# A one-element exponential ahead of the score exponentials, and the transposes of the smallest score tile moved behind the second vs product

## The chip, the cores and the metric

The kernel runs on one core of a Trainium2 chip. The metric is the device time of one execution in microseconds (us); a kernel's time is the median of several runs. Engines are named as in the profile: PE is TensorE's matrix multiplication and PEld its weight load, ACT is ScalarE, DVE is VectorE, POOL is GpSimd, SP is SyncE, which here issues most of the DMAs.

## What is computed

Three stages follow each other for 8 batches of 576 tokens with 512 features, all in float32:

```python
# 1: attention in two steps, 8 heads of 64
p_packed = sm_attn(p, k, v)                 # 32 packed queries per head
x = sm_attn(q, p_packed, p_packed)          # back to 576 tokens
# 2: a gated MLP that mixes tokens
h = gelu_tanh(x @ w_in)                     # 1024 features
u, v = h[..., :512], h[..., 512:]
v_n = (v - mean(v)) / sqrt(var(v) + 1e-6) * g_ln
v_s = einsum('ts,bsd->btd', w_sg, v_n) + b_sg
x = x + (u * v_s) @ w_out
# 3: four attention experts, causal; each token takes the best two of them by x @ w_gate
out = sum over experts of mask * w * (softmax(causal(q k^T / 8)) @ v) @ wo
```

## The kernel before, in words

Products that need accuracy are made of three passes over a high and a low part of each operand (`PASSES`), so PE has much to do. Tokens are cut into four tiles of 128 and one of 64 (`NT`, `TOK`). PSUM is one pool of four two-bank buffers (`pd`), which all products share.

Batches are worked in a software pipeline. `front(b)` makes the normalised v_n of batch b: it multiplies v out, runs gelu, mean and variance, scaling and the split into parts tile by tile, with the u products in between, and ends with `E0 E2`, which belong to the batch before: the scores and exponentials of stage 3. `later_back(b)` (batches 1 to 7) then makes the vs product (v_n with w_sg, four column tiles m of five parts c each) and the gate u * vs of batch b, interleaved with the rest of the attention of batch b - 1, and afterwards the q, k, v of batch b's stage 3 and the packed attention of the next one.

The names of the steps of stage 3: E are scores, causal mask, maximum and exponentials; N is the scaling by the reciprocal of the sum and the expert's weight; T turns the result with PE transposes and copies it out of PSUM on ACT; y is the product with v; o is the output projection. For the first two query tiles both head pairs are done together: E0, N0 and T0 are the 128-column tile, E2, N2 and T2 the 256-column tile (`att_exp2`, `att_norm2`, `att_T2`). Line 1013 holds their score products, 1015 the mask, 1018 the maximum, 1022 the exponentials, 1028 and 1029 the sums, 1031 the scalings, and 1041 the transposes; their copy is recorded at the helper's line 82, as are all plain ACT copies. N0 has four scalings and T0 four transposes with one copy; N2 has four and T2 eight with two.

What sets the order: on PE and SP the order is that of the program text through the whole main loop. In `front` it is so on DVE and ACT as well (`tc.manual_schedule(engines={ET.DVE, ET.Activation})`). In `later_back` DVE and ACT are ordered by the planner of the framework, which simulates the program and takes the ready instruction that stands earliest in the text, save in the few blocks marked otherwise. Waits between engines are put in by the framework. ACT holds one table of functions at a time: gelu's or the exponential's; the load of a table is an instruction of its own that is put ahead of the first activation that needs it, and has that activation's line. Per batch there are two: at line 722 (gelu) and at line 1022 (exponential).

The last steps of `front` on ACT are the scaled copies of the 64-token tile into its high and low part (lines 747 and 749). `vs_part` (lines 820, 824, 826) makes one part c of one column tile m: six matmuls for c below 4 and four for c = 4. `vs_out` multiplies by u on DVE (843), copies the high part on ACT (849) and makes the low part on DVE (helper line 85). `mhalf` is a constant column of -0.5.

Of the kernel before, what the change touches and what calls it, by code (L numbers as in the profile page):

```python
# [7 lines left out]
F32 = mybir.dt.float32  # L8
# [5 lines left out]
AF = mybir.ActivationFunctionType  # L14
# [3 lines left out]
P = 128  # L18
# [8 lines left out]
def packed_attention_mlp_moe_kernel(  # L27
# [18 lines left out]
    nc = tc.nc  # L46
# [6 lines left out]
    NT = 5  # L53
# [5 lines left out]
    small = ctx.enter_context(tc.tile_pool(name="small", bufs=4))  # L59
# [14 lines left out]
    def pd(name):  # L74

        return psum.tile([P, 2, 512], F32, tag="pd", name=name, bufs=NPS)
# [10 lines left out]
    def hs(h):  # L87
        return slice(h * HALF, (h + 1) * HALF)
# [17 lines left out]
    mhalf = consts.tile([P, 1], F32, name="mhalf")  # L106
# [246 lines left out]
    def prep_w_o(j):  # L353
        hi, lo = W["w_o"]
        st = wst.pop(("o", j))
        act_copy(hi[:, j, :], st)
        lo_part(nc.vector, lo[:, j, :], st, hi[:, j, :])
# [27 lines left out]
    def tick(n=1):  # L385
        for _ in range(min(n, len(TURN))):
            for f in TURN.pop(0):
                f()
# [274 lines left out]
    def bdw(b):  # L663
        bdw_qk(b)
        bdw_vg(b)
# [23 lines left out]
    def v_mm(b, pt, c):  # L689
        s = ST[b]  # L690
        n = 0
        if c == 4:
            for y in range(2):
                for Q in range(2):
                    nc.tensor.matmul(pt, s["a2", Q][0][:, 512:640], wp_part(b, 1, y, Q), start=n == 0, stop=n == 3)
                    n += 1
            return
        for x, y in PASSES:
            for Q in range(2):
                nc.tensor.matmul(pt, s["a2", Q][x][:, c * P:(c + 1) * P], wp_part(b, 1, y, Q), start=n == 0, stop=n == 5)  # L700
                n += 1

    def v_gelu(b, pt, c):
        if c == 4:
            v_sum_high(b, pt)
            v_sum_low(b, pt)
            v_sum_gelu(b)
            return
        vg = ST[b]["vg", c] = slot("t", w=512, name="vg")
        nc.scalar.activation(vg, pt, AF.Gelu_apprx_tanh)  # L710

    def v_sum_high(b, pt):
        vg = ST[b]["vg", 4] = slot("t", w=512, name="vg")[:64]
        act_copy(vg, pt[64:])

    def v_sum_low(b, pt):
        vg = ST[b]["vg", 4]
        nc.vector.tensor_tensor(vg, vg, pt[:64], op=OP.add)

    def v_sum_gelu(b):  # L720
        vg = ST[b]["vg", 4]
        nc.scalar.activation(vg, vg, AF.Gelu_apprx_tanh)
# [80 lines left out]
    def vs_tile(b, m):  # L803
        vs_mm(b, m)
        vs_out(b, m)

    def vs_mm(b, m):
        for c in range(NT):
            vs_part(b, m, c)

    def vs_part(b, m, c):
        s = ST[b]
        cols = slice(m * P, (m + 1) * P)
        if c == 0:
            s["vs", m] = pd("vs")[:, :, :HALF]
        pt = s["vs", m]
        if c < 4:
            for x, y in PASSES:
                for h in range(2):
                    nc.tensor.matmul(pt[:, h, :], s["vn", c][x][:, cols], w_sg[y][:, c, hs(h)],  # L820
                                     start=(c, x, y) == (0, 0, 0), stop=False)
            return
        for h in range(2):
            nc.tensor.matmul(pt[:, h, :], s["vn", 4][0][:, cols], w_sg[0][:, 4, hs(h)], start=False, stop=False)
        for h in range(2):
            nc.tensor.matmul(pt[:, h, :], s["vn", 4][1][:66, cols], w_sg[1][:66, 4, hs(h)], start=False, stop=True)
# [7 lines left out]
    def vs_out(b, m):  # L834
        gate_mul(b, m)
        gate_high(b, m)
        gate_low(b, m)
# [18 lines left out]
    def qk(b, i):  # L856
        qk_mm(b, i)
        qk_out(b, i)
# [6 lines left out]
    def qk_gated(b, i, first, ms=range(4)):  # L865
        s = ST[b]
        if first:
            s["qkp", i] = pd("qk")[:, :, :HALF]
        o = s["qkp", i]
        cols = slice(i * P, (i + 1) * P)  # L870
        for m in ms:
            for x, y in PASSES:
                for h in range(2):
                    nc.tensor.matmul(o[:, h, :], W["w_qk"][y][:, m, cols], s["g", m][x][:, hs(h)],  # L874
                                     start=first and (m, x, y) == (0, 0, 0), stop=not first and (m, x, y) == (3, 1, 0))

    def qk_packed(b, i, first):
        s = ST[b]
        if first:
            s["qkp", i] = pd("qk")[:, :, :HALF]  # L880
        o = s["qkp", i]
        cols = slice(i * P, (i + 1) * P)
        for Q in range(2):
            for x, y in PASSES:
                for h in range(2):
                    nc.tensor.matmul(o[:, h, :], s["bd", Q][y][:, cols], s["a2", Q][x][:, hs(h)],  # L886
                                     start=first and (Q, x, y) == (0, 0, 0), stop=not first and (Q, x, y) == (1, 1, 0))
# [12 lines left out]
    def keep_last_q(b, pr):  # L900
        for z, t in zip(last_q[pr], ST[b]["qk", pr]):
            for e in range(2):
                r = slice(64 * e, 64 * e + 64)
                nc.gpsimd.tensor_copy(z[r, r], t[r, 4 * P:S])

    def gate_beside(b):
        for m in range(4):
            t = ST[b]["gx", m]
            nc.gpsimd.tensor_copy(t[:, S:S + 64], t[:, 2 * S:])  # L909
# [309 lines left out]
    def weights(b, names):  # L1219
        if b < B:  # L1220
            for n in names:
                load_w(n)

    def front(b, go):

        with tc.manual_schedule(engines={ET.DVE, ET.Activation}):
            p4 = pd("v")[:, 0, :]
            v_mm(b, p4, 4)
            v_sum_high(b, p4)
            tick()  # L1230
            p = [None] * 4
            for c in range(4):
                if c % 2 == 0:
                    t = pd("v")
                p[c] = t[:, c % 2, :]
                v_mm(b, p[c], c)
                if c == 1:
                    v_sum_low(b, p4)
                    v_sum_gelu(b)
                    tick()  # L1240

            def run(names):
                fs = dict(g=lambda b, c: v_gelu(b, p[c], c), b=v_stats, p=v_pow, c=v_scale, h=v_high, l=v_low, U=u_mm,
                          u=u_gelu)
                for n in names.split():
                    if n == "t":
                        tick()
                    else:
                        fs[n[0]](b, int(n[1]))

            run("b4 g0 g1 b0 p0 c0 b1 p1 c1 h0 l0 U0 t")
            run("g2 g3 b2 p2 h1 c2 u0 l1 U1 t b3 p3 p4 c3 u1 U2 t h2 l2 u2 U3 t c4 h3 l3 u3 h4 l4")
            go("E0 E2")

    def second(b, do_all):
        do_all("r")
        for f in (1, 0):
            wp_mm(b, f)
        for f in (1, 0):
            wp_out(b, f)  # L1260
# [28 lines left out]
    def later_back(b, go, do_all, nxt):  # L1289
        go("N0 N2")  # L1290
        vs_tile(b, 0)
        for c in range(3):
            vs_part(b, 1, c)
        go("T0")
        for c in range(3, NT):
            vs_part(b, 1, c)
        with tc.manual_schedule(engines={ET.Activation}):
            go("T2")
            vs_out(b, 1)
        go("y0")  # L1300
        if b == 1:
            for j in range(2):
                prep_w_o(j)
        go("S5 S4")
        vs_tile(b, 2)
        go("o0 y1 T5 T4 S6 S7")
        vs_tile(b, 3)
        tick(len(TURN))
        if b + 1 < B:
            STEP.pop((b + 1, "f"))()  # L1310
        go("o1 y2")
        bdw(b)
        weights(b + 1, ("in1", "in0"))
        qk(b, 0)
        do_all("V T6 o2 T7 K0 S8 S9 K1")
        keep_last_q(b, 0)
        gate_beside(b)
        qk_gated(b, 2, True)
        with tc.manual_schedule(engines={ET.DVE}):
            do_all("s0 s1 n0 n1")  # L1320
        qk_packed(b, 2, False)
        qk_out(b, 2)
        if b + 1 == B:
            go("y3 T8 T9 o3 y4")
            nxt("E8")
            go("o4")
            vlog(b, VT[1])
            nxt("E6")
            vlog(b, VT[2])
            nxt("E4")  # L1330
            return
        do_all("y3 T8 T9 o3 a0 a1 y4 pp Q0 Q1 o4 P0 P1")
        vlog(b, VT[1])
        second(b + 1, do_all)
        vlog(b, VT[2])
        if b + 2 < B:
            ahead(b + 2)
# [43 lines left out]
    def ahead(b):  # L1381

        do(p1_steps(b))
# [255 lines left out]
    with tc.manual_schedule(engines={ET.PE, ET.SP}):  # L1639
        go = back(0, attention(-1))  # L1640
        for b in range(1, B):
            front(b, go)
            go = back(b, go)
# [31 lines left out]
```

## Time and profile before

| | us |
|---|---|
| median of 3 runs (lowest to highest) | 823.51 (823.33 to 825.58) |
| the profiled execution | 824.52 |
| its span, first to last instruction | 822.8 |
| PE busy in the span | 792.6 |
| DVE, ACT, POOL busy in the span | 586.8, 428.4, 229.3 |

The profile is of one execution. Times in it run from the start of the span. In a row of the timeline the columns are start, length, engine, line and operation, with the output and the input; rows of several instructions (x4) give the time from the start of the first to the end of the last. What stands in brackets is the idle time of the engine just before, and the instruction that ended it. The ends of matmuls are modelled, so their starts are the better marks.

### The profile page before, as it was taken

Reading aid. Unit: us, or ns where it says so; the run is one execution under the profiler, and the core shown is the slowest. Engines: PE = TensorE matmul, PEld = TensorE weight load, DVE = VectorE, ACT = ScalarE, POOL = GpSimd, SP = SyncE. Lnnn points to the kernel's source line nnn. Section 1 sums busy time; section 2 is a strip of 40 time slices with the busy share of each in tenths; the row PEclk is TensorE's granted clock in tenths of the full one; section 3 lists DMA queues with packets and bytes.
Section 4 is the critical chain, followed back from the end, with each engine's and each line's share of the span. In section 5 each row is a group of like instructions: output and inputs, shape, how many; then the busy total and the mean of one; then the engine's idle time right before and its main releaser. Section 6 shows DMA issues by size and latency. Waiting matters only on the chain.

```text
span 822.8 us, 19132 instructions
## 1 busy us (share of the span) xinstructions
PE 792.6 (96%) x7459; PEld 689.4 (84%) x7459; DVE 586.8 (71%) x1321; ACT 428.4 (52%) x947; POOL 229.3 (28%) x346
## 2 busy tenths in 40 slices
PE   4789899999999999999999999999999999999998
PEld 2457778988899888988899888988899888988886
DVE  4898567886488756886488757886488747885383
ACT  3566343665347543665347543575347543565454
POOL 2356443403331222403331222403331232300000
PEclk9979999999999999999999999999999999999999
DMA  9977889507582475607682476607672372000001
GB/s 236 292 201 166 241 252 228 142 14 223 153 196 73 102 232 158 161 18 221 149 199 74 105 231 173 149 15 221 155 194 73 97 238 85 1 15 26 21 1 58
DMA packets 172709, 114.99 MB, mean 140 GB/s; under 512 B 119306, under 2 KB 153610, under 8 KB 169804
## 3 DMA queue, kind: packets, MB, share of 16 engines
q1 hardware_dynamic: 165644, 112.19, 50.5%
q10 hardware_dynamic: 6976, 1.58, 0.9%
q8 instruction: 59, 0.97, 0.5%
q14 instruction: 30, 0.25, 0.1%
HBM read 69.18 MB, written 29.63 MB: 120 GB/s over the span
## 4 chain that ended last, share of the span: by engine, by line
PE 71%; DVE 12%; ACT 9%; DMA 3%; issue 3%; POOL 1%; SPq 0%; ACTq 0%; DVEq 0%; POOLq 0%
PE qk L874 13%; PE vs L820 7%; PE y L1124 7%; PE qk L886 6%; PE o L1173 5%; PE vlog L933 5%; PE aTp L1095 3%; PE sc L991 3%; PE vlog L937 3%; DVE bnst L728 2%; PE s L395 2%; ACT vnh L747 2%; DMA k<-in_k_dram 2%; PE aTp L1041 2%; PE sc L1068 2%
## 5 line engine op out<-in xcount | busy, mean ns | idle before, releaser
L874 PE MATMUL qk<-g,w_qk 128*128 128x288 f32 x768 | 107.4, 297 | 0.4 <-ACT a L490 0.4
L874 PEld LDWEIGHTS qk<-g,w_qk 128*128 128x128 f32 x768 | 103.4, 189 | 4.3 <-issue 2.9
L820 PE MATMUL vs<-w_sg,vnh 128*128 128x288 f32 x512 | 92.0, 302 | 1.5 <-ACT vs L82 1.5
L820 PEld LDWEIGHTS vs<-w_sg,vnh 128*128 128x128 f32 x512 | 74.8, 189 | 8.3 <-issue 5.6
L82 ACT ACTIVATE aT<-aTp 128x512 f32<-128x512 f32 (+4 forms) x125 | 55.8, 512 | 18.0 <-PE aTp L1041 9.1
L909 POOL CAST g<-g 128x64 fp32r<-128x64 f32 x32 | 9.0, 284 | 195.2 <-DVE g L85 93.3
L482 POOL COPY qT<-qp 128x576 uint16<-128x576 uint16 x56 | 43.0, 838 | 60.6 <-DMA qp<-turned_q 60.5
L1124 PE MATMUL y<-aT,v 128*64 128x128 f32 (+2 forms) x960 | 58.3, 263 | 1.0 <-ACT aT L82 0.9
L1001 ACT ACTIVATE at<-sc,nm 128x384 f32<-128x384 f32 (+3 forms) x72 | 43.4, 609 | 30.2 <-DVE nm L995 26.3
L1124 PEld LDWEIGHTS y<-aT,v 128*64 128x64 f32 (+1 forms) x960 | 46.8, 136 | 13.3 <-issue 8.3
L820 PE MATMUL vs<-w_sg,vnl 128*128 128x288 f32 x256 | 54.7, 295 | 0.0
L933 PE MATMUL vlog<-w_vg,g 128*128 128x260 f32 x384 | 52.1, 285 | 0.0
L736 POOL TENSOR_TENSOR rstd<-rstd,mhalf 128x1 f32<-128x1 f32 (+1 forms) x40 | 34.7, 868 | 56.8 <-DVE rstd L732 46.9
L1173 PE MATMUL o<-w_o,y 128*128 128x512 f32 x186 | 49.4, 401 | 0.0
L933 PEld LDWEIGHTS vlog<-w_vg,g 128*128 128x128 f32 x384 | 48.4, 189 | 1.2 <-PE wp L620 0.8
L482 POOL COPY kT<-kp 128x576 uint16<-128x576 uint16 x56 | 44.7, 876 | 8.9 <-DMA kp<-turned_k 8.9
L886 PE MATMUL qk<-a2h,bdq 128*128 128x288 f32 x256 | 45.4, 299 | 0.5 <-DVE sm L548 0.4
L820 PEld LDWEIGHTS vs<-w_sg,vnl 128*128 128x128 f32 x256 | 41.0, 188 | 0.0
L886 PEld LDWEIGHTS qk<-a2h,bdq 128*128 128x128 f32 x256 | 37.2, 188 | 4.5 <-issue 3.9
L85 DVE TENSOR_TENSOR y<-y 128x256 fp32r<-128x256 f32 (+1 forms) x40 | 15.9, 397 | 33.8 <-ACT y L1137 33.8
L1173 PEld LDWEIGHTS o<-w_o,y 128*128 128x128 f32 x186 | 32.9, 188 | 5.9 <-issue 0.5
L995 DVE TENSOR_REDUCE nm<-sc 128x2 f32<-128x768 f32 (+3 forms) x36 | 37.1, 1030 | 1.0
(264 smaller groups left out, 1895.6 us busy)
## 6 DMA issues: line engine op xcount, KB each, us to landing
w_in<-kept_in SPq DMA_DIRECT2D x14, 1024.0 KB
w_qk<-kept_qk SPq DMA_DIRECT2D x8, 1024.0 KB
turned_k<-kx SPq DMA_DIRECT2D x28, 288.0 KB
turned_q<-qx SPq DMA_DIRECT2D x28, 288.0 KB
kp<-turned_k SPq DMA_DIRECT2D x56, 144.0 KB
qp<-turned_q SPq DMA_DIRECT2D x56, 144.0 KB
out_dram<-ot SPq DMA_DIRECT2D x31, 256.0 KB
v<-in_v_dram SPq DMA_DIRECT2D x56, 128.0 KB
```

The costliest lines, as they stand in the source:

```text
L82: nc.scalar.activation(o, i, AF.Copy, scale=scale)
L482: nc.gpsimd.tensor_copy(w[:, i], t[:, i].rearrange("p h n -> p (h n)"))
L736: nc.gpsimd.tensor_tensor(rstd, rstd, mhalf[:TOK[c]], op=OP.pow)
L820: nc.tensor.matmul(pt[:, h, :], s["vn", c][x][:, cols], w_sg[y][:, c, hs(h)], start=(c, x, y) == (0, 0, 0), stop=False)
L874: nc.tensor.matmul(o[:, h, :], W["w_qk"][y][:, m, cols], s["g", m][x][:, hs(h)], start=first and (m, x, y) == (0, 0, 0), stop=not first an ...
L886: nc.tensor.matmul(o[:, h, :], s["bd", Q][y][:, cols], s["a2", Q][x][:, hs(h)], start=first and (Q, x, y) == (0, 0, 0), stop=not first and ...
L933: nc.tensor.matmul(pt[:, ci, :260], s["g", m][x][:, c * P:c * P + P], W["w_vg"][y][:, m, :], start=(m, x, y) == (0, 0, 0), stop=False)
L937: nc.tensor.matmul(pt[:, ci, :260], s["a2", Q][x][:, c * P:c * P + P], s["bdv", Q][y], start=False, stop=(Q, x, y) == (1, 1, 0))
L995: nc.vector.tensor_reduce(nm, pt[:, :, :L], axis=AX.X, op=OP.max, negate=True)
L1001: nc.scalar.activation(ats[e][:, :L], pt[:, e, :L], AF.Exp, bias=nm[:, e:e + 1], accum_out=sm[:, e:e + 1])
L1124: nc.tensor.matmul(pt[64 * e:64 * e + 64, pr * w:pr * w + w], s["v2"][:m, c, col:col + D], s["aT", pr, e, j][c][:m, :], start=c == 0, stop ...
L1173: nc.tensor.matmul(pt, ys[:, pr, x, :], W["w_o"][y][:, pr, :], start=i == 0, stop=i == 5)
```

## The change

Two edits. Behind the steps of the 64-token tile in `front` and ahead of the exponentials of E0, ACT computes an exponential of one column with one element per partition (`mhalf`), whose result nobody reads. In `later_back`, the transposes T0, which stood between the third and the fourth part of the second vs product (m = 1), come behind its fifth part, directly ahead of T2, and their copy stands with that of T2 in the block whose ACT order is that of the text.

```diff
             run("g2 g3 b2 p2 h1 c2 u0 l1 U1 t b3 p3 p4 c3 u1 U2 t h2 l2 u2 U3 t c4 h3 l3 u3 h4 l4")
+            warm = small.tile([P, 2], F32, name="st3")[:, 0:1]
+            nc.scalar.activation(warm, mhalf, AF.Exp)
             go("E0 E2")
...
     def later_back(b, go, do_all, nxt):
         go("N0 N2")
         vs_tile(b, 0)
-        for c in range(3):
-            vs_part(b, 1, c)
-        go("T0")
-        for c in range(3, NT):
-            vs_part(b, 1, c)
+        vs_mm(b, 1)
         with tc.manual_schedule(engines={ET.Activation}):
-            go("T2")
+            go("T0 T2")
             vs_out(b, 1)
         go("y0")
```

## Rows read from the trace of the kernel before

**Rows 1.** The page: busy time by engine, and PE's granted clock in 40 slices.

```profile
PE 792.6 (96%) x7459; PEld 689.4 (84%) x7459; DVE 586.8 (71%) x1321; ACT 428.4 (52%) x947; POOL 229.3 (28%) x346
...
PEclk9979999999999999999999999999999999999999
```

**Rows 2.** Waits of PE (total, times, longest): whole run, then 253 to 346 us.

```profile
PE aTp L1041 <- DVE at L1031: 2.7, 7, 0.4
...
PE aTp L1041 <- DVE at L1031: 0.4, 1, 0.4
```

**Rows 3.** Busy time by stretch: stretch, length, then PE, PEld, DVE, ACT, POOL, clock.

```profile
253.00:345.00 92.00, 91.56 (x908) 81.42 (x906) 66.50 (x153) 48.77 (x108) 25.07 (x42) 1.00 0.53 145
```

**Rows 4.** Timeline of ACT from 257 to 263 us.

```profile
257.32 1.28 ACT L1022 ACT_TABLE_LOAD   x1 [1.70 <-DVE nm L1018]
258.62 0.37 ACT L1022 ACTIVATE at<-sc,nm 128x128 f32<-128x128 f32 x1
...
260.00 0.49 ACT L1022 ACTIVATE at<-sc,nm 128x256 f32<-128x256 f32 x1
...
261.35 0.51 ACT L1022 ACTIVATE at<-sc,nm 128x256 f32<-128x256 f32 x1
261.80 0.72 ACT L849 ACTIVATE g<-gt 128x576 fp32r<-128x576 f32 x1
262.38 0.64 ACT L82 ACTIVATE aT<-aTp 128x512 f32<-128x512 f32 x1
```

**Rows 5.** Timeline of DVE from 257 to 264 us.

```profile
257.89 1.23 DVE L1018 TENSOR_REDUCE nm<-sc 128x4 f32<-128x1024 f32 x1
259.03 0.75 DVE L843 TENSOR_TENSOR gt<-vs,u 128x576 f32<-128x576 f32 x1
260.16 0.17 DVE L1028 TENSOR_SCALAR sm<-sm 128x4 f32<-128x4 f32 x1 [0.39 <-ACT at L1022]
...
260.58 1.12 DVE L1031 TENSOR_SCALAR at<-at,sm,gw 128x128 f32<-128x128 f32 x4
261.99 0.17 DVE L1028 TENSOR_SCALAR sm<-sm 128x4 f32<-128x4 f32 x1 [0.29 <-ACT at L1022]
...
262.41 1.38 DVE L1031 TENSOR_SCALAR at<-at,sm,gw 128x256 f32<-128x256 f32 x4
```

**Rows 6.** Timeline of PE from 260 to 265 us.

```profile
260.23 0.43 PE L820 MATMUL vs<-w_sg,vnl 128*128 128x288 f32 x2
261.07 1.01 PE L1041 MATMUL aTp<-ident,at 128*128 128x128 f32 x4 [0.41 <-DVE at L1031]
261.83 0.77 PE L820 MATMUL vs<-w_sg,vnh 128*128 128x288 f32 x4
...
263.24 1.04 PE L1041 MATMUL aTp<-ident,at 128*128 128x128 f32 x8
264.21 0.66 PE L1124 MATMUL y<-aT,v 128*64 128x128 f32 x8
```

**Rows 7.** Timeline of PE, the same step in the first of the seven batches.

```profile
168.55 1.01 PE L1041 MATMUL aTp<-ident,at 128*128 128x128 f32 x4 [0.27 <-DVE at L1031]
```

**Rows 8.** Timeline of ACT at 235 us: the exponential of the gates.

```profile
235.31 0.22 ACT L968 ACTIVATE gw<-gw 128x20 f32<-128x20 f32 x1 [4.23 <-DVE gw L967]
```

**Rows 9.** Timelines of DVE and PE at 272 us: the 384-column tiles.

```profile
271.61 0.87 DVE L1056 TENSOR_SCALAR at<-at,sm,gw 128x384 f32<-128x384 f32 x2
...
272.37 1.53 PE L1095 MATMUL aTp<-ident,at 128*128 128x128 f32 x12
```

**Rows 10.** Timeline of ACT at 241 us, then the group of all gelu loads (busy, mean ns, idle before).

```profile
241.05 0.59 ACT L82 ACTIVATE vg<-v 64x512 f32<-64x512 f32 x1 [0.33 <-PE v L695]
241.66 1.28 ACT L722 ACT_TABLE_LOAD   x1
...
L722 ACT ACT_TABLE_LOAD x7 | 9.0, 1283 | 0.1
```

## Prediction

> **What bounds the kernel now.** I read the page first: TensorE (PE) is busy for 96% of the span, and its granted clock is at full speed in all but the first slices [rows 1]. What sets the end is therefore PE's own queue, and a change helps only where PE is held up or does less. Next I read the waits of PE: in a whole steady batch there is one group only, the transposes of line 1041 waiting for line 1031, which occurs seven times in the run, once in each batch from the second on [rows 2]. The table by stretch agrees: of 92 us PE lacks 0.44 us [rows 3]. So almost the only thing this kernel could win without cutting PE work lies at this one place, and the change is aimed exactly there.
>
> Third, I laid the timelines of the three engines over each other at this place in the batch that runs around 260 us. On ScalarE (ACT) the load of the function table for the exponential starts at 257.32, after 1.70 us in which ACT was idle, and lasts 1.28 us; only then do the four exponentials of the 128-column score tile start (258.62), and those of the 256-column tile follow them (260.00, the last at 261.35) [rows 4]. On VectorE (DVE) the sums of the first tile are taken up at 260.16 after a wait of 0.39 us for ACT, its four scalings run from 260.58 to 261.70; the sums of the second follow at 261.99 after 0.29 us more, and its scalings end at 263.79 [rows 5]. PE issues the last two matmuls of the third part of the second vs product at 260.23 and then nothing until the first transpose at 261.07; parts four and five (ten matmuls) follow at 261.83, the eight transposes of the second tile at 263.24, and the y product at 264.21 [rows 6]. The table load thus stands on the path: maximum, load, exponentials, scalings, transposes.
>
> The loss of PE there is larger than the 0.41 us shown as idle. Ten matmuls take 263.24 − 261.83 = 1.41 us, 0.14 us each, so the first transpose could have issued at 260.23 + 0.28 = 260.51: 0.56 us are lost before it. Its four transposes last 0.76 us where eight take 0.97 us (four: 0.49), because they are handed out by the scalings one by one: 0.27 us more. Together 0.83 us a batch. In the first of the seven the idle is 0.27 instead of 0.41 us [rows 7], so 0.69 there.
>
> **Part 1: the one-element exponential.** It adds one ACT instruction in each of seven batches, behind the scaled copies of the 64-token tile and ahead of the exponentials, in an order that is fixed by hand. It reads a constant. The number of table loads stays the same: the load should move ahead of the new instruction, which has no maximum to wait for. ACT is then free at 257.32 − 1.70 = 255.62; the load ends at 255.62 + 0.02 + 1.28 = 256.92. The trace has no one-element activation. From below its cost can't be under nothing, since it is one more instruction on ACT; from above, the nearest row is the 128x20 exponential of the gates at 0.22 us [rows 8]; I take 0.22, as the fixed part must be most of so small an operation. ACT is ready at about 257.15, before the maximum lets it go at 257.30. The cover is 0.15 us; without it the instruction would cost up to 0.22 us a batch. What is queued behind it on ACT are only the exponentials, and their reader is the DVE step already followed here.
>
> The first four exponentials then start at 257.32 instead of 258.62, 1.30 us earlier, and last 1.38 us up to the next tile. That tile's maximum ends on DVE at 257.89 + 1.23 = 259.12 [rows 5], so its exponentials start at about 259.16 instead of 260.00: 0.84 us earlier, no more. Of the 1.28 us that are taken off the path, 0.44 us is thus lost to the second maximum, which is late next.
>
> On DVE: the multiplication of tile 0 (line 843) runs 259.03 to 259.78; the next instruction overlaps a finished one by some 0.08 us (259.03 against 257.89 + 1.23 shows 0.09). So the first sums are taken up at 259.70 instead of 260.16 (0.46 earlier), the scalings end at 261.24, and the second sums start at the later of 261.16 (DVE) and 261.99 − 0.84 = 261.15 (ACT): 0.83 us earlier. The lower bound is the two idle times alone, 0.39 + 0.29 = 0.68; the upper is ACT's 0.84. The second tile's scalings then end at 262.96 instead of 263.79.
>
> **Part 2: transposes of the first tile moved behind parts four and five.** No instruction is added or removed. The ten matmuls now start at 260.51 and end at 261.92; the four transposes, ready since 261.24, run at PE's own rate until 262.41; the eight follow. What is given up: the ten matmuls stood between the first and the second tile's transposes and covered the second tile's scalings; now nothing does. The eight transposes can't end before their last scaling: before, y started 263.79 → 264.21, 0.42 us behind it. With the end at 262.96, y starts at 263.38. By PE alone it would be 262.41 + 0.97 = 263.38, the same time; both bounds give 0.83 us. If the last two transposes follow their scaling more quickly than 0.42 us (0.34 would be 0.14 for the hand-over, as 260.58 + 0.34 to 261.07 shows it, and two transposes), 0.1 us more; if DVE gains only its idle times, 0.68.
>
> The copy of the first tile's transposes, now in the fixed ACT order, moves with them. Before it started at 262.38, straight behind the copy g [rows 4]; now the transposes end at about 262.5, the copy takes 0.64 us and y needs it at 263.38: cover 0.2 us. The g copy is by then done, since the exponentials ahead of it end 0.84 us earlier. No DMA is issued in the moved steps. On PE, the y product, the next two score tiles and the third vs product are queued behind the transposes. DVE's and ACT's work there (second gate, y, the next maxima) hangs on the same events and moves along. The next transposes that could be late are the 384-column ones: they start at 272.37 while the last scaling for them runs until 271.61 + 0.87 = 272.48 [rows 9]. That scaling belongs to the second half of the twelve, which comes 0.73 us later, so about 0.6 us of slack; if DVE didn't move at all, 0.83 − 0.6 = 0.2 us a batch would be given back there.
>
> **Sum.** I take 0.80 us for six batches and 0.70 for the first: 5.5 us. The profiled execution took 824.52 us (822.8 us of span and 1.7 around it), so 819.0; the median of the runs shown is 1.0 us lower (823.51), so 818.0. Own range of this case: 0.6 us a batch (4.2 us, 819.3) to 0.93 (6.5 us, 817.0).
>
> **A rule against it.** Where a load follows directly on another ACT instruction, the trace shows no gap: the copy of line 82 ends at 241.05 + 0.59 = 241.64 and the load of the gelu table starts at 241.66; over seven such loads the idle ahead of them is 0.1 us [rows 10]. The Trainium skill (ScalarE: Activation LUTs, section "What ACT_TABLE_LOAD costs") gives a switch 1283 ns for the load, which this trace agrees with (1283), and about 1380 ns of drain besides, which no row here shows. In the present place such a drain could have been hidden in the 1.70 us of idle; behind the change it would lie open, and the load would start 1.38 us later, at 257.02.
>
> **The rivals.** (a) The early load gains next to nothing, because something must pass on ACT between the last copy and the load, hidden today in the idle. With 1.38 us there (the figure of that page), ACT would be ready at 258.30 + 0.22 = 258.52 against 258.62: 0.1 us a batch, 0.7 in all, 822.8. Against it: the gelu loads, which have no such gap. The same result comes if the load stays where it is; then only part 2 acts, and y still waits for the second scalings' end, 263.79 + 0.42: 823.5. Chance of both: 0.08. (b) One 0.75 us DVE instruction comes to lie ahead of the second tile's sums, since DVE's order in this stage isn't written by hand but planned: gain 0.83 − 0.75 = 0.1, again about 823. Chance 0.07. (c) The other side: that instruction is the multiplication of the second vs product (line 843). It couldn't have been there before, as its last ten matmuls came behind the first transposes; now the product is complete before them. But it ends on PE only at 261.92; DVE would sit still, multiply until 262.75, and take up the second sums there instead of at 261.99: 0.76 us later than before, and y with them. Seven times: 5.3 us, 828.8. It decides when the planner believes the second sums later than 261.92; in truth they are ready at 261.15, and the program names the scalings of both tiles first. Chance 0.10.
>
> **How the numbers follow.** Forecast 0.75, no gain (a, b) 0.15, slower 0.10. 0.3% of this time, about what a measurement of this kernel can tell from no change, is 2.5 us; the forecast's whole own range lies beyond it. So faster 0.75, same 0.15, slower 0.10. The range reaches from the best case (816.8) to the rivals without gain (823.5); only (c) is left out.
>
> **What would show it.** Right: the load of line 1022 stands at the new line with no idle before it, ending about 256.9 on the present scale; the exponentials follow the maximum within 0.05 us; the wait of line 1041 for line 1031 is gone or below 0.1 us; y of the first tile starts 0.8 us earlier relative to the scores of line 1013. A load that begins over 1 us after the last copy shows (a); line 843 twice ahead of the second pass through line 1028 shows (c). A new wait of line 1095 for line 1056, or of y for the copy of the first transposes, would mean that the gain was given back behind this place.

## The result and the profile after

The changed kernel takes 816.78 us (median of 4 runs, 816.48 to 818.06) against 824.5 us for four runs of the kernel before; the ratio is 0.991 with a 95% interval of 0.9889 to 0.9931, so 5.7 to 9.1 us faster. Taken once more beside the experiments below it was 816.86 against 823.13 us, ratio 0.9937 (0.9922 to 0.9951): 4.0 to 6.4 us.

The chain of work that ended last, in one line of each page. The page of the kernel before:

```profile
PE 71%; DVE 12%; ACT 9%; DMA 3%; issue 3%; POOL 1%; SPq 0%; ACTq 0%; DVEq 0%; POOLq 0%
```

The page of the changed kernel, its busy times first:

```profile
PE 786.2 (96%) x7459; PEld 686.0 (84%) x7459; DVE 585.8 (72%) x1321; ACT 430.7 (53%) x954; POOL 229.2 (28%) x346
...
PE 88%; DVE 5%; DMA 4%; ACT 1%; issue 1%; SPq 1%; POOL 0%; ACTq 0%; DVEq 0%; POOLq 0%
```

PE executes the same 7459 matmuls; DVE and ACT have left the chain between about 140 and 790 us, where it now runs through PE alone but for two pieces of 0.03 us. The line tells the path and not the size of the gain: the page of the kernel with the new instruction alone, below, has PE 88%; DVE 5% as well, though it gains less. PE's wait for line 1031 [rows 2] is no longer in the table of waits at all, and of the 92 us of [rows 3] PE now lacks 0.03 us instead of 0.44:

```profile
253.00:345.00 92.00, 91.97 (x913) 82.00 (x912) 67.17 (x154) 49.20 (x110) 25.75 (x41) 1.00 0.56 153
```

Now the same stretch as [rows 4], ACT in the changed kernel (start, length, instruction, idle before in brackets):

```profile
253.26 0.71 ACT L749 ACTIVATE vnl<-vg,rstd 64x512 fp32r<-64x512 f32 x1
253.99 1.28 ACT L1254 ACT_TABLE_LOAD   x1
255.28 0.20 ACT L1254 ACTIVATE st<-mhalf 128x1 f32<-128x1 f32 x1
255.69 0.37 ACT L1022 ACTIVATE at<-sc,nm 128x128 f32<-128x128 f32 x1 [0.20 <-DVE nm L1018]
...
257.55 0.47 ACT L1022 ACTIVATE at<-sc,nm 128x256 f32<-128x256 f32 x1 [0.36 <-DVE nm L1018]
...
259.36 0.69 ACT L849 ACTIVATE g<-gt 128x576 fp32r<-128x576 f32 x1
260.82 0.60 ACT L82 ACTIVATE aT<-aTp 128x512 f32<-128x512 f32 x1 [0.77 <-PE aTp L1041]
```

The load has moved to the new line and starts 0.02 us behind the last copy, where it stood idle for 1.70 us before. The exponentials of both tiles now wait for their maximum and for nothing else. DVE there, against [rows 5]:

```profile
256.23 1.23 DVE L1018 TENSOR_REDUCE nm<-sc 128x4 f32<-128x1024 f32 x1
257.37 0.75 DVE L843 TENSOR_TENSOR gt<-vs,u 128x576 f32<-128x576 f32 x1
258.04 0.16 DVE L1028 TENSOR_SCALAR sm<-sm 128x4 f32<-128x4 f32 x1
...
258.44 1.12 DVE L1031 TENSOR_SCALAR at<-at,sm,gw 128x128 f32<-128x128 f32 x4
259.51 0.17 DVE L1028 TENSOR_SCALAR sm<-sm 128x4 f32<-128x4 f32 x1
...
259.93 1.38 DVE L1031 TENSOR_SCALAR at<-at,sm,gw 128x256 f32<-128x256 f32 x4
```

Both waits of line 1028 are gone, and DVE runs through these steps without a gap. PE, against [rows 6]:

```profile
259.92 0.43 PE L826 MATMUL vs<-w_sg,vnl 66*128 66x288 f32 x2
260.19 1.62 PE L1041 MATMUL aTp<-ident,at 128*128 128x128 f32 x12
261.74 0.66 PE L1124 MATMUL y<-aT,v 128*64 128x128 f32 x8
```

The twelve transposes follow the second vs product at once. The y product still starts 0.43 us behind the end of the second scalings (259.93 + 1.38 = 261.31), as it did before (0.42): DVE's chain still reaches y as late as PE's queue does, although the chain of the page names PE alone here. As a clock for the stage I use the time from the first score product of line 1013 to the first y product. In this batch it is 261.74 − 251.06 = 10.68 us here and 264.21 − 252.72 = 11.49 before:

```profile
252.72 1.64 PE L1013 MATMUL sc<-qk 64*128 64x128 f32 x24
```

```profile
251.06 1.64 PE L1013 MATMUL sc<-qk 64*128 64x128 f32 x24
```

Over the seven batches the difference is 0.78, 0.81, 0.82, 0.83, 0.81, 0.80 and 0.82: 5.67 us. From each y to the next line 1013, and from the last y to the end, the kernels agree (0.1 us more and 0.2 us less in all). The remaining 0.76 us of the 6.5 us between the two spans lie ahead of the first score product, which starts at 160.34 before and at 159.58 after. That part of the program is the same in both; over the ten profiles of this study it ended between 157.43 and 161.02.

### The profile page after: what moved, and what is told of

It reads as the page before. It is cut to its first block, busy times and chain, and to the rows that moved or that the text cites. A ratio compares the mean times of both kernels' runs of the same rounds, so it can differ in the third digit from the quotient of the medians.

```text
span 816.3 us, 19139 instructions
## 1 busy us (share of the span) xinstructions
PE 786.2 (96%) x7459; PEld 686.0 (84%) x7459; DVE 585.8 (72%) x1321; ACT 430.7 (53%) x954; POOL 229.2 (28%) x346
## 4 chain that ended last, share of the span: by engine, by line
PE 88%; DVE 5%; DMA 4%; ACT 1%; issue 1%; SPq 1%; POOL 0%; ACTq 0%; DVEq 0%; POOLq 0%
PE qk L874 13%; PE vs L820 12%; PE y L1124 7%; PE qk L886 6%; PE u L790 6%; PE o L1173 5%; PE v L700 5%; PE vlog L933 5%; PE aTp L1095 3%; PE sc L991 3%; PE vlog L937 2%; PE s L395 2%; PE fold L324 2%; PE sc L1068 2%; PE wp L620 2%; PE sc L1013 1%
## 5 line engine op out<-in xcount | busy, mean ns | idle before, releaser
L1124 PEld LDWEIGHTS y<-aT,v 128*64 128x64 f32 (+1 forms) x960 | 46.8, 136 | 13.3 <-issue 8.1
L995 DVE TENSOR_REDUCE nm<-sc 128x2 f32<-128x768 f32 (+3 forms) x36 | 37.1, 1031 | 1.0
```

The costliest lines, as they stand in the source:

```text
L995: nc.vector.tensor_reduce(nm, pt[:, :, :L], axis=AX.X, op=OP.max, negate=True)
L1124: nc.tensor.matmul(pt[64 * e:64 * e + 64, pr * w:pr * w + w], s["v2"][:m, c, col:col + D], s["aT", pr, e, j][c][:m, :], start=c == 0, stop ...
```

## The experiments

**The halves and the whole.** The first takes only this from the change:

```diff
+            warm = small.tile([P, 2], F32, name="st3")[:, 0:1]
+            nc.scalar.activation(warm, mhalf, AF.Exp)
             go("E0 E2")
```

> The one-element exponential alone; the transposes of the first tile stay behind the third part of the second vs product. Theory (the load is on the path through maximum, exponentials, scalings): the first sums are taken up 0.46 us earlier, but the first transposes stand between parts three and four and still wait for their scalings, so PE gets back about 0.47 of the 0.83 us a batch: 3.3 us in all, 0.4%. Rival (the load costs nothing because the second maximum is late anyway, and the order of the transposes is what counts): within 0.5 us of before.

Measured: 819.31 us against 823.13, ratio 0.9964 (0.9953 to 0.9975), 2.1 to 3.9 us faster; the stage takes 11.01 us, 0.48 less. PE in this kernel:

```profile
258.84 0.43 PE L820 MATMUL vs<-w_sg,vnl 128*128 128x288 f32 x2
259.20 1.00 PE L1041 MATMUL aTp<-ident,at 128*128 128x128 f32 x4
259.96 0.77 PE L820 MATMUL vs<-w_sg,vnh 128*128 128x288 f32 x4
```

The wait is too short now to be shown as idle (0.08 us by the prediction's working, from 258.84 + 0.28 to 259.20), but the four transposes still take 0.76 us, as in [rows 6]: they are still handed out by the scalings.

The second takes the other part alone:

```diff
-        for c in range(3):
-            vs_part(b, 1, c)
-        go("T0")
-        for c in range(3, NT):
-            vs_part(b, 1, c)
+        vs_mm(b, 1)
         with tc.manual_schedule(engines={ET.Activation}):
-            go("T2")
+            go("T0 T2")
```

> The moved transposes alone; the load stays at the first exponential. Theory: the wait at line 1041 gets shorter or goes over to the second tile, but y of the first tile still starts 0.42 us behind the end of the second scalings, which don't move: 0 us, at most 0.1 us a batch (0.7 us in all). Rival (PE's gain comes from the order: no stall in the middle of the vs product and one change of kind of work less): 0.5 to 0.8 us a batch, 3.5 to 5.6 us.

Measured: 822.49 us against 823.13, ratio 0.9997 (0.9985 to 1.0008): no change that can be told; the stage takes 11.50 us, as before. PE in this kernel, and the second scalings on DVE:

```profile
258.94 0.60 PE L1041 MATMUL aTp<-ident,at 128*128 128x128 f32 x4
260.06 1.32 PE L1041 MATMUL aTp<-ident,at 128*128 128x128 f32 x8 [0.52 <-DVE at L1031]
261.31 0.66 PE L1124 MATMUL y<-aT,v 128*64 128x128 f32 x8
...
259.50 1.38 DVE L1031 TENSOR_SCALAR at<-at,sm,gw 128x256 f32<-128x256 f32 x4
```

The first four transposes no longer wait. The wait has gone over to the second tile whole, and y starts when it started before: 0.43 us behind the end of the second scalings (260.88).

> Both parts, the changed kernel once more, on the same chip as the two halves. Theory: 5.7 us (seven times 0.81, as the two profiles show between the scores of line 1013 and y), which is 2 us more than the sum of the halves; what was measured beyond that (6.5 us between the spans) came from the first 160 us and differs from run to run. Rival (the gain is 7 to 8 us, something else in the kernel got faster too): 7 us or more with the whole interval.

Measured: the 0.9937 given above, 4.0 to 6.4 us, with 10.67 us for the stage. The sum from the stage, 5.67, lies inside, and 7 us lies outside. The first comparison alone (5.7 to 9.1 us) would have allowed 7; two of its four runs of the kernel before, 825.48 and 825.58 us, are at the top of what the 23 runs here show (821.05 to 825.58), so its larger figure need not mean a second gain. Load alone 0.48 us a batch, order alone 0.00, both 0.81: the order is worth 0.33, but only once the second scalings come earlier.

**The slower rival: a multiplication ahead of the second sums.** Two kernels. In both, DVE's order is written by hand; the first:

```diff
-        go("N0 N2")
-        vs_tile(b, 0)
-        vs_mm(b, 1)
+        with tc.manual_schedule(engines={ET.DVE}):
+            vs_mm(b, 0)
+            gate_mul(b, 0)
+            go("N0")
+            gate_high(b, 0)
+            vs_mm(b, 1)
+            gate_mul(b, 1)
+            go("N2")
+        gate_low(b, 0)
         with tc.manual_schedule(engines={ET.Activation}):
             go("T0 T2")
-            vs_out(b, 1)
+            gate_high(b, 1)
+        gate_low(b, 1)
```

> Both parts, and in each of the seven batches the multiplication of the second vs product (line 843) is put by hand ahead of the second tile's sums on DVE, the case (c) of the prediction. Theory: DVE waits for the end of that product on PE and multiplies first; the second scalings end 1.5 us later than in the changed kernel, y with them: 10 to 11 us slower than the changed kernel, about 4 to 6 us slower than before. Rival (DVE has room, and the order on it doesn't matter within this stage): within 1 us of the changed kernel.

Measured: 835.35 us against 823.13, ratio 1.0157 (1.0141 to 1.0174); 18.5 us slower than the changed kernel (816.86), more than expected. Two reasons are in the trace. The low part of the first gate, which was left out of the block, had been put by the planner between the first scalings and the multiplication, so two DVE instructions and a wait stood ahead of the second sums:

```profile
263.43 0.76 DVE L85 TENSOR_TENSOR g<-gt,g 128x576 fp32r<-128x576 f32 x1 [0.53 <-ACT g L849]
264.11 0.75 DVE L843 TENSOR_TENSOR gt<-vs,u 128x576 f32<-128x576 f32 x1
264.77 0.16 DVE L1028 TENSOR_SCALAR sm<-sm 128x4 f32<-128x4 f32 x1
```

And in some batches PE worked slowly behind the longer wait. Its timeline in one of them, then its stretches (length, PE, PEld, DVE, ACT, POOL, and the granted clock ahead of the last two columns):

```profile
263.53 0.60 PE L1041 MATMUL aTp<-ident,at 128*128 128x128 f32 x4
265.74 1.57 PE L1041 MATMUL aTp<-ident,at 128*128 128x128 f32 x8 [1.61 <-DVE at L1031]
267.24 1.12 PE L1124 MATMUL y<-aT,v 128*64 128x128 f32 x8
268.29 2.08 PE L991 MATMUL sc<-qk 64*128 64x384 f32 x12
```

```profile
263.00:265.60 2.60, 1.13 (x10) 0.89 (x8) 2.10 (x6) 1.00 (x2) 0.24 (x1) 1.00 0.00 0
265.60:270.40 4.80, 4.66 (x29) 3.48 (x29) 2.33 (x6) 1.93 (x4) 0.24 (x1) 0.64 0.01 3
270.40:275.00 4.60, 4.60 (x32) 4.48 (x33) 4.30 (x12) 2.47 (x8) 0.00 (x0) 1.00 0.00 0
```

Behind 1.61 us of idle the mean granted clock was 0.64 for 4.8 us, so mostly at the lower of its two levels (1.2 instead of 2.4 GHz), and from the start of y to the start of the third vs product it took 3.07 us instead of 1.83. This happened in three of the seven batches (around 266, 361 and 736 us). In the other four the clock stayed at 1.00 behind nearly the same idle, as here:

```profile
455.85 1.31 PE L1041 MATMUL aTp<-ident,at 128*128 128x128 f32 x8 [1.61 <-DVE at L1031]
...
455.60:460.40 4.80, 4.55 (x39) 3.69 (x40) 2.55 (x8) 1.93 (x4) 0.24 (x1) 1.00 0.00 0
```

In these four the stage takes 1.90 us more than in the changed kernel. Seven times that, 13.3 us, is the price of the order; the three falls of the clock make about 4 of the 18.4 us between the two profiled spans, an estimate from the time of the three stretches beside the same ones of the changed kernel. The remaining 1 us lies outside the stages. The second kernel names the low part behind the second scalings:

```diff
             gate_mul(b, 1)
             go("N2")
-        gate_low(b, 0)
+            gate_low(b, 0)
```

> As the run with the multiplication of the second vs product ahead of the second sums, but the low part of the first gate (0.75 us, which had come to lie ahead of it too) is named behind the second scalings. Theory: DVE multiplies when the vs product ends on PE, the second sums start 1.5 us later than in the changed kernel, y with them: 10.8 us slower than the changed kernel if PE keeps its clock in the idle of some 1.2 us that then lies between the two groups of transposes. In the first of these two runs PE was idle there for 1.61 us, the granted clock was 0.64 over the next 4.8 us, and 1.9 us a batch at y had become 2.6 us. If the clock falls behind 1.2 us too: about 15 us slower than the changed kernel.

Measured: 828.27 us against 823.65, ratio 1.0054 (1.0039 to 1.0069), 11.4 us slower than the 816.86 of the changed kernel, which was not timed again beside this run and the next three. In all seven batches PE was idle for 1.24 us and kept its clock. DVE, then PE, then the stretch behind the wait (granted clock 1.00):

```profile
261.74 0.76 DVE L843 TENSOR_TENSOR gt<-vs,u 128x576 f32<-128x576 f32 x1 [0.83 <-PE vs L826]
262.41 0.16 DVE L1028 TENSOR_SCALAR sm<-sm 128x4 f32<-128x4 f32 x1
```

```profile
263.38 1.32 PE L1041 MATMUL aTp<-ident,at 128*128 128x128 f32 x8 [1.24 <-DVE at L1031]
264.62 0.66 PE L1124 MATMUL y<-aT,v 128*64 128x128 f32 x8
```

```profile
264.00:266.00 2.00, 2.00 (x21) 1.54 (x22) 0.86 (x2) 1.27 (x3) 0.24 (x1) 1.00 0.04 8
```

The stage takes 12.21 us, 0.72 more than before. So the rival's mechanism exists and has about the price given for it (0.76); the planner just didn't choose that order.

**How much cover the new instruction has.** The exponential repeated four and twelve times:

```diff
-            nc.scalar.activation(warm, mhalf, AF.Exp)
+            for _ in range(4):
+                nc.scalar.activation(warm, mhalf, AF.Exp)
```

> The changed kernel with four one-element exponentials in place of one. Theory: the exponentials of the first tile start up to 0.45 us later, but nothing waits for that, since the second tile's maximum lets ACT go 0.36 us after the first tile's are done, and DVE takes up the first sums 0.8 us after they are there: within 0.3 us of the changed kernel. Rival (the prediction's words: a cover of 0.15 us, and what is beyond it costs): 0.1 to 0.4 us a batch, 0.7 to 2.8 us in all.

Measured: 817.28 us against 823.65, ratio 0.9928 (0.9912 to 0.9943); the stage takes 10.68 us, as with one. ACT is now the later one for the first tile, and still the stage's end does not move:

```profile
254.37 0.91 ACT L1255 ACTIVATE st<-mhalf 128x1 f32<-128x1 f32 x4
255.19 0.35 ACT L1022 ACTIVATE at<-sc,nm 128x128 f32<-128x128 f32 x1
```

> The changed kernel with twelve one-element exponentials. Theory: eleven more of 0.11 to 0.2 us make ACT ready 1.2 to 2.2 us later, 1.0 to 2.0 us behind the first maximum; the second tile's exponentials, which follow the first's by 1.4 us at least, start 0.4 to 1.4 us later, and y with them: 3 to 10 us slower than the changed kernel. If this run is the same as the changed kernel too, ACT is not on the path at all and the theory falls.

Measured: 849.07 us against 823.65, ratio 1.0301 (1.0277 to 1.0324): 32 us slower than the changed kernel, not 3 to 10. The twelve take 2.81 us. But with them the planner also laid out another order on DVE: the second multiplication and a low part stand ahead of the second scalings. The twelve on ACT, then DVE:

```profile
256.36 2.81 ACT L1255 ACTIVATE st<-mhalf 128x1 f32<-128x1 f32 x12
...
262.44 0.17 DVE L1028 TENSOR_SCALAR sm<-sm 128x4 f32<-128x4 f32 x1 [0.30 <-ACT at L1022]
262.51 0.75 DVE L843 TENSOR_TENSOR gt<-vs,u 128x576 f32<-128x576 f32 x1
263.18 0.17 DVE L1029 RECIPROCAL sm<-sm 128x4 f32<-128x4 f32 x1
263.27 0.72 DVE L85 TENSOR_TENSOR g<-gt,g 128x576 fp32r<-128x576 f32 x1
263.91 1.37 DVE L1031 TENSOR_SCALAR at<-at,sm,gw 128x256 f32<-128x256 f32 x4
```

To tell the two apart, the same twelve with DVE's order held to that of the changed kernel:

```diff
-        go("N0 N2")
-        vs_tile(b, 0)
-        vs_mm(b, 1)
-        with tc.manual_schedule(engines={ET.Activation}):
-            go("T0 T2")
-            vs_out(b, 1)
+        with tc.manual_schedule(engines={ET.DVE}):
+            vs_mm(b, 0)
+            gate_mul(b, 0)
+            go("N0 N2")
+            gate_high(b, 0)
+            gate_low(b, 0)
+            vs_mm(b, 1)
+            with tc.manual_schedule(engines={ET.DVE, ET.Activation}):
+                go("T0 T2")
+                vs_out(b, 1)
```

> Twelve one-element exponentials as before, but with DVE's order in this stage held to that of the changed kernel (multiplication of tile 0, first sums and scalings, second sums and scalings, then the low part and the second multiplication). In the run before, the planner had put the second multiplication and the low part ahead of the second scalings, and PE had then been idle for 1.94 us with the granted clock at 0.82 and 0.75 behind it. Theory: what is left is ACT's delay; the second exponentials start 1.8 us later than in the changed kernel (260.45 against 257.55, the stage itself starting 1.08 us later there), y with them: 1.8 us a batch, 12.6 us slower than the changed kernel, 829 to 830 us, if the clock stays up in an idle of about 1.1 us. Rival (ACT's delay itself made most of the 32 us): above 840 us.

Measured: 830.03 us against 823.21, ratio 1.0081 (1.0064 to 1.0098), 13.2 us slower than the changed kernel; the stage takes 12.46 us, 1.79 more. The second exponentials on ACT, then PE:

```profile
260.45 0.48 ACT L1022 ACTIVATE at<-sc,nm 128x256 f32<-128x256 f32 x1
...
263.40 1.32 PE L1041 MATMUL aTp<-ident,at 128*128 128x128 f32 x8 [0.89 <-DVE at L1031]
264.65 0.66 PE L1124 MATMUL y<-aT,v 128*64 128x128 f32 x8
```

ACT's delay is worth what was expected, and behind 0.89 us of idle the clock stayed at 1.00 in all seven batches. The other 19 us of the run before came with the order, the clock that fell behind it included; the two were not taken apart.

## Why the prediction was right, point by point

**The bound.** That PE's queue sets the end and that this one wait is all it loses in a steady batch was right: with the wait gone, the gain stayed to the end in full, and no later step gave any of it back. The idle time in the table of waits (2.7 us in all, [rows 2]) would have promised half of it; that the transposes handed out one by one cost as much again was the prediction's own step, and 0.81 us a batch against its 0.83 bears it out. The 384-column transposes, for which 0.6 us of slack was worked out, show no new wait for line 1056.

**The load.** It moved to the new instruction, whose duration is 0.20 us against the 0.22 taken. On the stage's own clock (from line 1013) the first exponentials came 1.27 us earlier (4.63 against 5.90) and the second 0.79 us (6.49 against 7.28), where 1.30 and 0.84 were expected; that the second maximum would be late next is the 0.36 us of idle in the profile after. One sign was missed: the exponentials were to follow their maximum within 0.05 us, and the second tile's follow its end (256.23 + 1.23 = 257.46) by 0.09. The prediction's 0.04 at this place is where its 0.84 is 0.05 too high. The load alone gave 0.48 us a batch, as the first pass of DVE through its sums (0.46) had it.

**The order.** Right in both directions. Alone it gives nothing, because y hangs on the end of the second scalings; with the load moved up it adds 0.33 us. The two bounds of the prediction, by DVE and by PE, both gave 0.83 us; measured are 0.81. The sum was set at 0.80 and 0.70; the first batch, for which PE's smaller idle was taken as the bound, gained 0.78. So 5.5 was expected and 5.67 found in the stage.

**The rest of the time.** The predicted median of 818.0 is 1.2 us above the one measured, and 816.78 is faster than the best case of the prediction's sum (817.0; its later 816.8 does not follow from that sum). For the profiled executions 819.0 was expected and 818.06 came: of these 0.9 us the stage makes 0.2, and 0.76 lie ahead of 160 us, in a stretch that differs by up to 3.6 us between profiles of a program that is the same there. No step of the sum speaks of that stretch, so where the total fell is in part luck; the sum itself is tested by the 5.67 us of the stage. How the medians, of runs without a profile, divide is not shown.

**A cover that was mis-sized.** The prediction gave the new instruction 0.15 us of cover and up to 0.22 us a batch beyond it. Four of them cost nothing. What was left out is that the first tile's exponentials aren't the ones that bind: the second maximum lets ACT go 0.36 us later than it could, and DVE is busy with the second maximum and the multiplication of tile 0 until 0.8 us after the first exponentials are done. That cover was worked out only up to the next start on the same engine instead of up to the step that is late last.

**The rivals.** (a) fell by the profile after: 0.02 us lie between the last copy and the load, and 0.01 us between the load and the exponential behind it, so no drain of 1.38 us stands there, as none stood ahead of the gelu loads [rows 10]. The figure of the Trainium skill (ScalarE: Activation LUTs, section "What ACT_TABLE_LOAD costs") for the load itself agrees with these rows, the one for the drain doesn't. (b) and (c) didn't come about: DVE's order in this stage is the same as before. With twelve exponentials the planner did choose an order akin to (c), with the second multiplication ahead of the second scalings.

## What to carry to other kernels

When an engine must load a table before it may work on something that comes late, an instruction of one element that needs nothing late can take the load out of the chain, as it did here; what it is worth is the time up to the next thing that is late (here 0.48 us alone and 0.81 us with the transposes moved), not the 1.28 us of the load. Moving a waiting step behind other work on its own engine gave nothing here while the step after it waited for the same chain (0.00 us alone, 0.33 us once that chain was shorter), so such edits are to be timed alone and together. Where a planner lays out an engine's order, a few instructions added on another engine can change it, and that can cost more than the instructions: compare the orders first, then the times.

## What the runs showed of the hardware

Seven one-element exponentials show 0.20 us each, and twelve in a row take 2.81 us, so 0.24 us from one to the next. They don't overlap, where the exponentials of the first score tile start 0.34 to 0.36 us apart though one lasts 0.36 to 0.38. The twelve all write the same column; whether that is the reason is not shown.

A stall of PE can cost more than its length, but stalls of one length do not always do so. Behind each of the seven waits of 1.24 us the granted clock stayed at 1.00. Of the seven of the first kernel with a multiplication ahead of the second sums (1.49 us once, 1.60 to 1.61 six times), three were followed by the lower level. In the run with twelve exponentials and the planner's own order (1.94 to 1.95 us) six of seven were, and the first was not. So in the same place the fall came with the longer waits, and the length of the wait alone does not decide it; what else does is open. The stretches around one of the six show the clock (the column ahead of the last two):

```profile
262.00:266.00 4.00, 2.06 (x11) 1.63 (x10) 2.98 (x9) 1.47 (x4) 0.26 (x1) 0.82 0.01 4
266.00:270.00 4.00, 4.00 (x30) 3.18 (x29) 1.93 (x4) 1.93 (x4) 0.24 (x1) 0.75 0.00 0
```

The kernel before, with 0.27 to 0.41 us of idle in this place, never showed that: its clock there was 1.00 in all seven batches.
